# Row sums of a fused attention and SoLU kernel: 128x32 tiles of TensorE replaced by 64x64 tiles, and one PSUM copy per group of quads

## The chip, the cores and the metric

The kernel runs on one core of one Trainium2 chip. The metric is device time in microseconds (us) for one execution; the figure for a kernel is the median of several runs. The profile is one execution of its own, recorded by the hardware profiler, and its span is the time from the first to the last recorded event. Two of the chip's engines matter most below: TensorE (PE in the profile), which multiplies a stationary block of weights with a stream of moving columns and writes into the accumulator memory PSUM, and ScalarE (ACT), which takes exponentials and copies results out of PSUM. VectorE is DVE, GpSimd is POOL, SyncE is SP and issues most DMAs.

## The reference

Attention with normalised queries and keys, followed by a feed-forward block with a SoLU activation. For 8 batches of 12 heads, 448 tokens and 64 dimensions per head:

```
q_n, k_n = q / rms(q) * g_q, k / rms(k) * g_k
scores = q_n @ k_n.T / sqrt(64)
attn   = exp(scores - max) / (sum(exp(scores - max)) + 1e-9)     # sum over the keys
x      = attn @ v                                                # then (token, head*dim)
h      = x @ w_in                                                # 768 -> 1024
solu   = h * softmax(h);  ln = layernorm(solu) * g_ln
out    = ln @ w_out                                              # 1024 -> 768
```

Everything is float32. The change concerns only the sums over the keys, 8*12*448 numbers, by which the rows of the attention output are divided.

## The kernel before, in words

**Work and tiles.** The 96 heads are taken four at a time, a *quad*; there are 24 quads (`m` = 0 to 23), each with two pairs `i` of two heads `h`. For quads 1 to 23 the 448 keys are cut into seven blocks `kc` of 64. `both_scores` (line 870) makes the scores of one block for all four heads: four matmuls with 64 rows and 64 columns of weights and 448 moving columns (the queries), each in its own quarter of the 128x128 array, into one PSUM tile `s`. ScalarE turns the tile into exponentials `E` (the last block's are called `El`) in `exponentials` (line 833), with 128 partitions (64 keys of pair 0, then 64 keys of pair 1) times 2 heads times 448 queries. `both_values` (line 884) multiplies the same block by `v`, again four 64x64 matmuls, and accumulates over `kc` in the PSUM tile `o`. Quad 0 is built from other loads: its two pairs are taken one after the other in blocks of 128 keys (`scores`, `values`, lines 841 and 930), and only the last 64 keys of both share a tile (`scores_last`, `values_last`).

**Row sums.** The sums over keys are column sums of `E` over partitions. VectorE first adds some of the seven blocks elementwise into tiles `es` (`add_pair`, `add_to`), so that a quad has a short list of *terms*: five for quad 0, four for quads 1 and 2, three for each later quad (`El` and two `es`). Each term has a kind `w`: 2 means that its upper 64 partitions belong to pair 0 and its lower 64 to pair 1; 0 or 1 (quad 0 only) that all 128 belong to that pair. `sums` (line 941) lets TensorE do the rest with a stationary block of ones and zeros, `ones[:, w]`, of 128 rows and 32 columns: the first 16 columns give pair 0's sum and the last 16 pair 1's, each repeated 16 times. For each term there are four matmuls, one for each head `h` and each half `t` of the queries, with 224 moving columns, into four strips of 32 PSUM partitions.

`sums` runs once for a group of quads, nine times in all: after quad 0, after quads 1 and 2 together, and after each further three quads (`sums_at`, line 1458). I call each of the nine a *phase*. The quads of a phase land in different columns of the PSUM tile `sm`, so that `keep_sums` (line 957) needs one ScalarE copy for one or two quads and two copies for three, into `r`; one DMA then sends every sixteenth partition of `r` to DRAM (`sd`). Later the sums are loaded back, inverted and stored in `rd`, and `load_r` broadcasts them over the rows of x.

**What sets the order.** The whole order is written by hand in the body after line 1492. Each unit issues TensorE work, and the other engines' work stands between units. On TensorE a quad is four blocks of scores, then values and scores in turn, then four blocks of values. A phase of sums stands between the last values of a quad and the first scores of the next; in the phase after quads 1 and 2 a small transpose of the gains (`norm_gain`, line 477) follows the sums. `keep_sums` is called at the start of the next quad (line 1578), ahead of its exponentials on ScalarE; `send` comes after the DMAs that store the previous quad's output (line 1598). Three PSUM buffers of tag "t" are shared in turn by `s` and `sm` (and in the next stage by the products of `w_in`).

After the attention come the product with `w_in` (128x128 tiles, line 1103) with the activation behind it, and the product with `w_out` (line 1329), both by Strassen-like schemes on TensorE.

In the traces each matmul call of the code stands as two rows (float32 is streamed twice), so four calls are "x8".

Of the kernel before, what the change touches and what calls it, by code (L numbers as in the profile page):

```python
# [9 lines left out]
FP32 = mybir.dt.float32  # L10
# [356 lines left out]
def fast_path(  # L367
# [24 lines left out]
    nc = tc.nc  # L392
    B, H, S, D = q.shape
    DM, DFF = moe_w_in.shape
    P = 128
    NJ = S // P
# [24 lines left out]
    work = first.enter_context(tc.tile_pool(name="work", bufs=2))  # L421
# [1 line left out]
    w_out = conv = sums_in = None  # L423

    ident = consts.tile([P, P], FP32, name="ident")
    ones = work.tile([P, 3, 32], FP32, tag="ones", name="ones", bufs=1)

    w_in = {k: wi.tile([P, HD, DFF // 2], FP32, name=f"w_in{k}") for k in (0, 5, 1, 4, 3, 6, 2)}
    xd = [dram.tile([DM, S], FP32, name=f"xd{b}") for b in range(B)]
    sd = dram.tile([NQ, 8, S // 2], FP32, name="sd")  # L430
    rd = [dram.tile([NP // 2, 8, S // 2], FP32, name=f"rd{b}") for b in range(B)]
# [17 lines left out]
    def setup():  # L449
        nc.gpsimd.memset(mhalf, -0.5)  # L450
        nc.gpsimd.memset(seven, 7.0)
        nc.gpsimd.memset(eps, 1e-6)


        for i, x in enumerate((-1.9375, -1.00390625, -(0.1249 ** 2))):
            nc.gpsimd.memset(limits[:, i : i + 1], x)


        nc.gpsimd.memset(ones, 0.0)
        for i in range(2):  # L460
            c = slice(16 * i, 16 * i + 16)
            nc.gpsimd.memset(ones[:, i, c], 1.0)
            nc.gpsimd.memset(ones[i * D : (i + 1) * D, 2, c], 1.0)
        make_identity(nc, ident)

    def load_gains():
# [158 lines left out]
    st = {}  # L625
    quads = {}
# [303 lines left out]
    def values(n):  # L930


        d = st[n]
        for kc in range(NJ):
            for h in range(2):
                nc.tensor.matmul(
                    d["o"][h * D : (h + 1) * D, :], quads[n // 2]["v"][:, n % 2 + 2 * h, kc], d["E", kc][:, h],
                    start=False, stop=(kc == NJ - 1),
                )

    def sums(ms):


        sm = ps_t.tile([P, 2, 512], FP32, tag="t", name="sm")
        for j, m in enumerate(ms):
            terms = quads[m]["terms"]
            for x, (w, e) in enumerate(terms):
                for h in range(2):
                    for t in range(2):
                        g = 32 * (2 * h + t)  # L950
                        nc.tensor.matmul(  # L951
                            sm[g : g + 32, j % 2, j // 2 * S // 2 : (j // 2 + 1) * S // 2], ones[:, w], e[:, h, t * S // 2 : (t + 1) * S // 2],
                            start=(x == 0), stop=(x == len(terms) - 1),
                        )
        return sm

    def keep_sums(ms, sm):


        n = len(ms)  # L960
        r = work.tile([P, 3, S // 2], FP32, tag="r", name="r", bufs=1)
        w = min(n, 2)
        nc.scalar.copy(r[:, 0:w], sm[:, 0:w, 0 : S // 2])
        if n == 3:
            nc.scalar.copy(r[:, 2], sm[:, 0, S // 2 : S])

        def send():
            nc.sync.dma_start(sd[ms[0] : ms[0] + n].rearrange("j r c -> r j c"), r[0:P:16, 0:n])

        return send  # L970

# [46 lines left out]
    def load_r(g):  # L1018


        n = 2 if g == 0 else 1
        if g == 0:
            tiles = [work.tile([P, 2 * NB, 32], FP32, tag="qkn", name="r0", bufs=2).rearrange("p b d -> p (b d)") for _ in range(2)]
        else:
            tiles = [sums_in.tile([P, KD * 2 * P], FP32, tag="r", name="rg", bufs=1)]
        w = KD // n
        gs[g, "r"] = [x[:, 0 : w * 2 * P].rearrange("p (c t) -> p c t", c=w) for x in tiles]
        for i, x in enumerate(gs[g, "r"]):
            t = 2 * g * P
            while t < 2 * (g + 1) * P:  # L1030
                b, c = divmod(t, S)
                half, c = divmod(c, S // 2)
                k = min(S // 2 - c, 2 * (g + 1) * P - t)
                o = t - 2 * g * P
                for h in range(2):
                    r = rd[b].rearrange("j (h t i) c -> i t (j h) c", h=2, t=2, i=2)
                    r = r[h, half, i * w : (i + 1) * w, c : c + k]
                    nc.sync.dma_start(
                        x[h * D : (h + 1) * D, :, o : o + k], r.rearrange("c t -> () c t").to_broadcast([D, w, k])
                    )  # L1040
                t += k
# [181 lines left out]
    def in_parts():  # L1223
        def done(g, i):
            t = 2 * g + i
            ff_max(t)
            waits = {
                (NG - 2, 1): (1, 2, 3, 4, 5, 6), (NG - 2, 0): (2, 3, 4, 5, 6, 7.25),
                (NG - 1, 1): (1, 2, 4.5, 5, 7.25, 7.75), (NG - 1, 0): (2.25, 4.25, 5.25, 6, 7.5, 8.75),
            }.get((g, i), (1, 2, 3, 4, 5, 7) if i else (2, 3, 4, 6, 7, 9))  # L1230
            steps = (ff_exp, ff_mult, ff_deviations, ff_spread_of, ff_norm, ff_spread)
            for x, f in zip(waits, steps):
                later(x, lambda f=f: f(t))

        p = [products(g, lambda i, g=g: done(g, i)) for g in range(NG)]
        parts = [p[0][1], p[0][2]]
        for g in range(NG):
            turn = [p[g][6], p[g][5], p[g][7], p[g][4], p[g][3]]
            x = len(parts)
            if g + 1 < NG:  # L1240
                turn[4:] = [p[g + 1][1], p[g][3], p[g + 1][2]]
            parts += turn
            if g + 1 < NG:
                follow(parts, x + 1, lambda g=g: [scale(g + 1, i) for i in range(3)])
                if g + 2 < NG:
                    follow(parts, x + 2, lambda g=g: load_r(g + 2))
                    follow(parts, x + 3, lambda g=g: load_x(g + 2))
                follow(parts, x + 2, lambda g=g: sizes(g + 1))
                follow(parts, x + 2, lambda g=g: block_sums(g + 1, 0))
                follow(parts, x + (5 if g > 6 else 6), lambda g=g: block_sums(g + 1, 1))  # L1250
        return parts
# [189 lines left out]
    def unit(f, steps=4):  # L1441
        nonlocal now
        f()
        now += steps
        due = [x for x in todo if x[0] <= now]
        todo[:] = [x for x in todo if x[0] > now]
        for _, g in sorted(due, key=lambda x: x[0]):
            g()
# [23 lines left out]

    load_rows(0, (nc.sync, nc.sync, nc.scalar, nc.scalar))
    setup()
    load_gains()
    load_rows(1, (nc.sync, nc.sync, nc.scalar, nc.scalar))
# [15 lines left out]
    with tc.manual_schedule():  # L1492
# [53 lines left out]
        unit(lambda: values_last(0))  # L1546
        unit(lambda: values(0))
        unit(lambda: values(1))
        quads[0]["terms"] = [(2, quads[0]["E", NJ])]
        quads[0]["terms"] += [(0, st[0]["es"])] + [(1, st[1]["E", x]) for x in range(NJ)]  # L1550
        waiting = [0]

        def end_sums():
            sm = sums(waiting)
            return list(waiting), sm
# [5 lines left out]
        for m in range(1, NQ):  # L1561
            a, b = 2 * m, 2 * m + 1
# [14 lines left out]
            if kept:  # L1577
                sent = keep_sums(*kept)
                kept = None
# [132 lines left out]
            if m == NQ - 2:  # L1712
                load_x(0)
                load_r(0)
# [10 lines left out]
            if m in sums_at:  # L1725
                unit(lambda: None)
                kept = end_sums()
                waiting.clear()
        take(NQ - 1)
        sent = keep_sums(*kept)  # L1730
        store_x(NQ - 1)
        sent()
# [4 lines left out]
        parts_in = ExitStack()  # L1737
        sums_in = pool(parts_in, "sums_in")
        load_r(1)
        for _ in range(3):  # L1740
            load_next()
# [19 lines left out]
        for x in range(8, 44):  # L1761
            e = nc.vector if (44 + x) % 7 in (3, 5) else nc.gpsimd
# [28 lines left out]
        for n in range(NS):  # L1791
            base = period * n
            for i, name in enumerate(ORDER):
# [4 lines left out]
                x = HALVES[name][0]  # L1798
# [65 lines left out]
@with_exitstack  # L1864
def kernel(
    ctx: ExitStack,
    tc: tile.TileContext,
    q: bass.AP,
    k: bass.AP,
    v: bass.AP,  # L1870
    g_q: bass.AP,
    g_k: bass.AP,
    moe_w_in: bass.AP,
    moe_w_out: bass.AP,
    moe_g_ln: bass.AP,
    out: bass.AP,
):
    nc = tc.nc
    flags = ctx.enter_context(tc.tile_pool(name="flags", bufs=1))
    flag = flags.tile([1, 1], I32, name="flag")  # L1880
    large = flags.tile([1, 1], FP32, name="large")
    fast_path(tc, q, k, v, moe_w_in, moe_w_out, out, g_q, g_k, moe_g_ln, large)
    nc.vector.tensor_copy(flag, large)
    other = nc.values_load(flag[0:1, 0:1], min_val=0, max_val=1)
    with tc.If(other > 0):
        general_path(tc, q, k, v, g_q, g_k, moe_w_in, moe_w_out, moe_g_ln, out)
# [30 lines left out]
```

## Time and profile before

| | before |
|---|---|
| median of 3 runs | 782.74 us (782.05 to 783.13) |
| profiled execution, its own time | 781.84 us |
| its span | 780.0 us |
| PE busy | 771.0 us, 99% |
| DVE, ACT, POOL busy | 603.6, 508.9, 487.3 us |

A duration of one PE row is the time from its start to its modelled end; rows in different quarters of the array overlap, so what a group costs is read from the distance between the starts of groups. The chain of waits follows the work that ended last back to the start and so counts each moment once; its times stand some hundredths of a us off those of the timeline.

### The profile page before, as it was taken

The numbers are of one execution on the slowest core, as the hardware profiler recorded it, in microseconds if no ns is written. First come the engines' busy times: TensorE is split into PE (matmuls) and PEld (weight loads), VectorE is DVE, ScalarE is ACT, GpSimd is POOL, SyncE is SP. The second block draws the span as 40 slices with busy tenths as digits, with TensorE's granted clock in tenths as the row PEclk, the third lists the DMA queues.
The fourth block names the chain that finished last, engine by engine and source line by source line (L and its number), as shares of the span: only waits on it lengthen the run. The fifth ranks groups of instructions, "written<-read, shape, count | busy, mean of one in ns | idle before, by whom it ended". The sixth has DMA issues, their size and how long they took to land.

```text
span 780.0 us, 15087 instructions
## 1 busy us (share of the span) xinstructions
PE 771.0 (99%) x5262; PEld 478.3 (61%) x5262; DVE 603.6 (77%) x1064; ACT 508.9 (65%) x833; POOL 487.3 (62%) x635
## 2 busy tenths in 40 slices
PE   8999999999999999999999999999999999999997
PEld 4444445445454444444444444444899999999996
DVE  6878999999999983687777667685797695776844
ACT  6778898888989862787777656655626445464510
POOL 2565444455464552455687688888898787777862
PEclk9999999999999999999999999999999999999999
DMA  9999999999999367588887777773757647456312
GB/s 164 173 188 192 194 198 176 200 209 187 186 203 172 91 171 165 130 196 182 195 203 169 161 150 165 163 182 69 224 154 240 207 145 256 144 188 242 104 62 87
DMA packets 279818, 134.27 MB, mean 172 GB/s; under 512 B 190324, under 2 KB 264884, under 8 KB 279732
## 3 DMA queue, kind: packets, MB, share of 16 engines
q1 hardware_dynamic: 265892, 123.31, 70.4%
q10 hardware_dynamic: 13840, 9.90, 4.4%
q8 instruction: 44, 0.72, 0.4%
q14 instruction: 42, 0.34, 0.1%
HBM read 96.12 MB, written 37.04 MB: 171 GB/s over the span
## 4 chain that ended last, share of the span: by engine, by line
PE 94%; SPq 3%; DMA 1%; DVE 0%; POOL 0%; ACT 0%; issue 0%; POOLq 0%; ACTq 0%
PE A L1329 16%; PE o L891 15%; PE s L879 15%; PE A L1103 14%; PE B L1103 9%; PE B L1329 8%; PE D L1103 5%; PE C L1103 5%; PE C L1329 4%; PE sm L951 4%; SPq L647 2%; DMA qk<-in_k_dram 0%; DMA gg<-in_g_q_dram 0%; DVE part L696 0%; POOL ss L706 0%
## 5 line engine op out<-in xcount | busy, mean ns | idle before, releaser
L879 PE MATMUL s<-qkT 64*64 64x448 f32 x1288 | 139.3, 540 | 0.3 <-ACT qkT L745 0.2
L839 ACT ACTIVATE E<-s 128x896 f32<-128x896 f32 x144 | 124.5, 920 | 20.5 <-PE s L879 19.7
L729 POOL TENSOR_TENSOR qkn<-qk,ny 128x896 f32<-128x896 f32 x45 | 77.2, 1736 | 72.9 <-DVE ny L723 33.5
L891 PE MATMUL o<-E,v 64*64 64x448 f32 x1104 | 120.4, 536 | 0.0
L879 PEld LDWEIGHTS s<-qkT 64*64 64x64 f32 x1288 | 66.1, 191 | 60.0 <-issue 38.8
L1329 PE MATMUL A<-w_out,sums 128*128 128x192 f32 x392 | 79.8, 326 | 0.0
L1329 PE MATMUL B<-w_out,sums 128*128 128x192 f32 x392 | 79.8, 326 | 0.0
L891 PEld LDWEIGHTS o<-E,v 64*64 64x64 f32 x1104 | 42.4, 133 | 56.2 <-issue 49.0
L1103 PE MATMUL A<-w_in,xg 128*128 128x512 f32 x168 | 76.8, 593 | 0.0
L1103 PE MATMUL B<-w_in,xsum 128*128 128x512 f32 x168 | 76.7, 592 | 0.0
L1329 PEld LDWEIGHTS B<-w_out,sums 128*128 128x128 f32 x392 | 66.4, 190 | 0.0
L1329 PEld LDWEIGHTS A<-w_out,sums 128*128 128x128 f32 x392 | 66.4, 190 | 0.0
L750 DVE STREAM_TRANSPOSE qkT<-qkn 128x896 f32<-128x896 f32 x46 | 49.9, 1098 | 9.4 <-POOL qkn L729 9.4
L1103 PEld LDWEIGHTS B<-w_in,xsum 128*128 128x128 f32 x168 | 31.9, 190 | 40.2 <-issue 39.9
L1103 PEld LDWEIGHTS A<-w_in,xg 128*128 128x128 f32 x168 | 31.8, 190 | 40.1 <-issue 38.4
L905 DVE TENSOR_TENSOR es<-es,E 128x896 f32<-128x896 f32 x44 | 49.3, 1120 | 4.4
L1205 ACT ACTIVATE u<-u,shift,he 128x1024 f32<-128x1024 f32 x28 | 34.8, 1241 | 27.2 <-POOL shift L1201 27.1
L696 DVE TENSOR_REDUCE part<-sq 128x28 f32<-128x896 f32 x46 | 47.9, 1074 | 4.3 <-ACT sq L690 4.3
L1079 POOL TENSOR_TENSOR xsum<-xg 128x384 f32<-128x384 f32 x14 | 14.4, 1030 | 57.2 <-ACT xsum L1062 35.0
L899 DVE TENSOR_TENSOR es<-E 128x896 f32<-128x896 f32 x46 | 50.1, 1089 | 0.0
L1329 PE MATMUL A<-w_out,s 128*128 128x192 f32 x224 | 45.6, 326 | 0.0
L690 ACT ACTIVATE sq<-qk 128x896 f32<-128x896 f32 x45 | 41.0, 944 | 2.1 <-DMA qk<-in_k_dram 0.7
(173 smaller groups left out, 1655.4 us busy)
## 6 DMA issues: line engine op xcount, KB each, us to landing
ur<-ud SPq DMA_DIRECT2D x60, 256.0 KB, 4.7
ud<-ub SPq DMA_DIRECT2D x112, 128.0 KB, 2.8
xd<-xo SPq DMA_DIRECT2D x48, 224.0 KB, 4.2
qk<-in_q_dram SPq DMA_DIRECT2D x92, 112.0 KB, 4.2
qk<-in_k_dram SPq DMA_DIRECT2D x92, 112.0 KB, 4.0
v<-in_v_dram SPq DMA_DIRECT2D x23, 448.0 KB, 5.2
out_dram<-P SPq DMA_DIRECT2D x19, 384.0 KB, 4.0
raw<-in_moe_w_in_dram SPq DMA_DIRECT2D x12, 512.0 KB, 5.0
```

The lines of the kernel that those rows point to most:

```text
L690: nc.scalar.activation(d["sq"].rearrange("p (s b) d -> p s (b d)", s=2), d["qk"], AF.Square)
L696: nc.vector.tensor_reduce(norms[m]["part"][:, i], st[n]["sq"], AX, OP.add)
L729: e.tensor_tensor(d["qkn"].rearrange("p (s b) d -> p s b d", s=2), d["qk"].rearrange("p s (b d) -> p s b d", d=32), y.rearrange("p (s b) - ...
L750: nc.vector.transpose(d["qkT"].rearrange("p s t -> p (s t)"), d["qkn"].rearrange("p b d -> p (b d)"))
L839: nc.scalar.activation(e, s[:, :, 0:S], AF.Exp)
L879: nc.tensor.matmul(s[i * D : (i + 1) * D, h, 0:S], qkT[hh, i, 1, keys], qkT[hh, i, 0], start=True, stop=True)
L891: nc.tensor.matmul(d["o"][h * D : (h + 1) * D, i, 0:S], d["v"][pp, h, kc], d["E", kc][pp, h], start=kc == 0, stop=kc == NK - 1,)
L899: nc.vector.tensor_tensor(e, d["E", x], d["E", y], OP.add)
L905: engine.tensor_tensor(e, e, d["E", x], OP.add)
L1103: nc.tensor.matmul(k[bank], a[:, c], w_in[i][:, c], start=begin and c == 0, stop=c == HD - 1, skip_group_check=not begin,)
L1205: nc.scalar.activation(d["u"], d["u"], AF.Identity, scale=d["e"], bias=d["shift"])
L1329: nc.tensor.matmul(k[bank], a[:, c].rearrange("p a i -> p (a i)"), w_out[:, area, i, c], start=begin and c == 0, stop=c == KC - 1, skip_gr ...
```

## The change

The sums are made with the array tiling of scores and values. The stationary block is now 64 columns wide, and it is cut out of `ones` (112 columns, of which 48 to 63 are ones) at a place that depends on the quad's position `j` in its phase: its 16 columns of ones are columns 16j to 16j+15 of the block. So each quad of a phase writes its sums to PSUM rows of its own, and adds zeros to the others' rows; all quads of a phase accumulate in the same columns of `sm`. A term of kind 2 is four matmuls of 64 rows and 64 columns with 448 moving columns (head `h`, pair `i`), each pair in its own PSUM bank; a term of kind 0 or 1 (quad 0) is two matmuls of 128 rows and 64 columns. `keep_sums` makes one copy of 128 x 896 elements in every phase; `r` has no buffer of its own any more but takes its turn among the six `es` buffers. Two DMAs, one for each head, send the sums, and `load_r` reads the rows in the new order. GpSimd's setup has one memset of ones in place of four. For quad 0 the term `El` comes last instead of first.

```
-    ones = work.tile([P, 3, 32], FP32, tag="ones", name="ones", bufs=1)
+    ones = work.tile([P, 112], FP32, tag="ones", name="ones", bufs=1)
...
         nc.gpsimd.memset(ones, 0.0)
-        for i in range(2):
-            c = slice(16 * i, 16 * i + 16)
-            nc.gpsimd.memset(ones[:, i, c], 1.0)
-            nc.gpsimd.memset(ones[i * D : (i + 1) * D, 2, c], 1.0)
+        nc.gpsimd.memset(ones[:, 48:64], 1.0)
...
         sm = ps_t.tile([P, 2, 512], FP32, tag="t", name="sm")
+        runs = []
         for j, m in enumerate(ms):
-            terms = quads[m]["terms"]
-            for x, (w, e) in enumerate(terms):
+            w = ones[:, 48 - 16 * j : 112 - 16 * j]
+            for pair, e in quads[m]["terms"]:
                 for h in range(2):
-                    for t in range(2):
-                        g = 32 * (2 * h + t)
-                        nc.tensor.matmul(
-                            sm[g : g + 32, j % 2, j // 2 * S // 2 : (j // 2 + 1) * S // 2], ones[:, w], e[:, h, t * S // 2 : (t + 1) * S // 2],
-                            start=(x == 0), stop=(x == len(terms) - 1),
-                        )
+                    if pair < 2:
+                        runs.append((h, pair, w, e[:, h]))
+                        continue
+                    for i in range(2):
+                        pp = slice(i * D, (i + 1) * D)
+                        runs.append((h, i, w[pp], e[pp, h]))
+        for x, (h, i, w, e) in enumerate(runs):
+            same = [y for y, r in enumerate(runs) if r[:2] == (h, i)]
+            nc.tensor.matmul(sm[h * D : (h + 1) * D, i, 0:S], w, e, start=x == same[0], stop=x == same[-1])
         return sm
...
-        r = work.tile([P, 3, S // 2], FP32, tag="r", name="r", bufs=1)
-        w = min(n, 2)
-        nc.scalar.copy(r[:, 0:w], sm[:, 0:w, 0 : S // 2])
-        if n == 3:
-            nc.scalar.copy(r[:, 2], sm[:, 0, S // 2 : S])
+        r = work.tile([P, 2, S], FP32, tag="es", name="r", bufs=6)
+        nc.scalar.copy(r, sm[:, :, 0:S])
...
-            nc.sync.dma_start(sd[ms[0] : ms[0] + n].rearrange("j r c -> r j c"), r[0:P:16, 0:n])
+            rows = sd[ms[0] : ms[0] + n].rearrange("j (h r) c -> h j (r c)", h=2)
+            for h in range(2):
+                nc.sync.dma_start(rows[h], r[h * D : h * D + 16 * n : 16].rearrange("j i t -> j (i t)"))
...
-                    r = rd[b].rearrange("j (h t i) c -> i t (j h) c", h=2, t=2, i=2)
+                    r = rd[b].rearrange("j (h i t) c -> i t (j h) c", h=2, t=2, i=2)
...
-        quads[0]["terms"] = [(2, quads[0]["E", NJ])]
-        quads[0]["terms"] += [(0, st[0]["es"])] + [(1, st[1]["E", x]) for x in range(NJ)]
+        quads[0]["terms"] = [(0, st[0]["es"])] + [(1, st[1]["E", x]) for x in range(NJ)]
+        quads[0]["terms"] += [(2, quads[0]["E", NJ])]
```

The order of the instructions on TensorE, ScalarE and SyncE can be read from the two built kernels (lines between 459 and 955 stand up to three lines higher or some lines lower in the changed file; x4 is four calls).

TensorE around quad 0's phase, before; `vl` and `v` are values, `sm` the sums:

```order
L849 MATMUL s<-qkT 64x448 x12
L925 MATMUL o<-El,vl 64x448 x4
L936 MATMUL o<-E,v 64x448 x12
L951 MATMUL sm<-El,ones 32x224 x4
L951 MATMUL sm<-es,ones 32x224 x4
L951 MATMUL sm<-E,ones 32x224 x12
L879 MATMUL s<-qkT 64x448 x16
```

The same place in the changed kernel:

```order
L846 MATMUL s<-qkT 64x448 x12
L922 MATMUL o<-El,vl 64x448 x4
L933 MATMUL o<-E,v 64x448 x12
L955 MATMUL sm<-es,ones 64x448 x2
L955 MATMUL sm<-E,ones 64x448 x6
L955 MATMUL sm<-El,ones 64x448 x4
L876 MATMUL s<-qkT 64x448 x16
```

`El` has gone from the head of the sums to their end, and the 20 calls of 32 x 224 have become 12 of 64 x 448. In the later phases nothing changes its place: each term keeps its four calls, with 64 x 448 in place of 32 x 224.

ScalarE around the first phase of three quads, before; `sq` are squares for a later quad, `r` the copied sums:

```order
L714 ACTIVATE ny<-ny 128x56
L690 ACTIVATE sq<-qk 128x896 x2
L963 COPY r<-sm 128x448
L965 COPY r<-sm 128x224
L839 ACTIVATE E<-s 128x896 x5
L538 ACTIVATE tmp<-raw,seven 128x512
```

The same place in the changed kernel:

```order
L711 ACTIVATE ny<-ny 128x56
L687 ACTIVATE sq<-qk 128x896 x2
L963 COPY r<-sm 128x896
L836 ACTIVATE E<-s 128x896 x5
L535 ACTIVATE tmp<-raw,seven 128x512
```

Two copies of 672 elements per partition together have become one of 896, at the same place ahead of the exponentials.

## Prediction

> **What bounds the kernel now.** I read the page's busy times and its chain by engine first, then a table of windows, then the groups of the sums' line, then the chain and the timeline around the phases.
>
> ```profile
> span 780.0 us, 15087 instructions
> PE 771.0 (99%) x5262; PEld 478.3 (61%) x5262; DVE 603.6 (77%) x1064; ACT 508.9 (65%) x833; POOL 487.3 (62%) x635
> PE 94%; SPq 3%; DMA 1%; DVE 0%; POOL 0%; ACT 0%; issue 0%; POOLq 0%; ACTq 0%
> ```
>
> TensorE is busy for 771.0 of 780.0 us and makes 94% of the chain that ended last. A busy TensorE could still be one that idles inside a stage, so here is the bulk of the attention stage, in the table of windows (window, its length, then the busy time of PE, PEld, DVE, ACT and POOL, the granted clock, the DMA share and GB/s):
>
> ```profile
> 121.60:295.00 173.40, 173.39 (x1973) 84.46 (x1969) 160.26 (x206) 146.37 (x201) 89.63 (x118) 1.00 0.90 178
> ```
>
> TensorE idles 0.01 us in 173.40, at clock 1.00. The other engines have slack. Whatever TensorE is given more to do in this stage, it does on the critical path.
>
> The sums' line in the groups by form (tiles, shape, count, then busy time and mean ns of one):
>
> ```profile
> L951 PE MATMUL sm<-es,ones 128*32 128x224 f32 x376 | 22.2, 352 | 0.0
> L951 PE MATMUL sm<-El,ones 128*32 128x224 f32 x192 | 13.7, 357 | 0.0
> L951 PE MATMUL sm<-E,ones 128*32 128x224 f32 x40 | 2.4, 352 | 0.0
> ```
>
> That is 608 rows, 8 for each term: 76 terms (5 for quad 0, 2 x 4, 21 x 3). How fast a term goes shows in the timeline of TensorE at the first phase of three quads, and in the chain (start, length, what; the first and the last of the six such phases inside the stage, and two stretches of scores with no sums ahead of them):
>
> ```profile
> 81.83 0.93 PE L891 MATMUL o<-El,v 64*64 64x448 f32 x8
> 82.69 0.59 PE L951 MATMUL sm<-El,ones 128*32 128x224 f32 x8
> 83.10 0.94 PE L951 MATMUL sm<-es,ones 128*32 128x224 f32 x16
> 83.85 0.56 PE L951 MATMUL sm<-El,ones 128*32 128x224 f32 x8
> ```
>
> ```profile
> 82.76 3.54 PE sm L951 x72
> 86.31 3.23 PE s L879 x32
> ...
> 97.05 3.01 PE s L879 x32
> ...
> 107.58 3.01 PE s L879 x32
> ...
> 259.43 3.54 PE sm L951 x72
> 262.97 3.23 PE s L879 x32
> ```
>
> Two terms of the old sums take 83.85 - 83.10 = 0.75 us, so one takes 0.375. A group of four 64x64 matmuls with 448 columns, which is what scores and values are, takes 3.01 / 4 = 0.7525 us. Both run four tiles side by side at the same rate for each column; the old tiles simply have half the columns.
>
> **The main term: the stream.** In the new form a term of kind 2 is four 64x64 matmuls with 448 columns: the tiling, the shape and the mapping (64 rows of one pair, 64 columns of one head, one PSUM bank for each pair) of `both_values`. I therefore charge 0.7525 us in place of 0.375. The 64 columns of weights hold 16 of use and the array is held twice as long.
>
> **What goes with the old tiling.** At both ends of a phase there is a gap where the tiling changes. The last values of the quad start at 81.83 and need 0.7525, so the sums could start at 82.58 and start at 82.69: 0.11 us. The first term takes 0.41 instead of 0.375. The scores behind the phase take 3.23 in the chain, and 3.01 where no sums are ahead of them: 0.22. The whole phase costs 3.54 + 3.23 - 3.01 = 3.76 us, of which 9 x 0.375 = 3.38 are stream and 0.38 the two changes.
>
> For these gaps the Trainium skill has a rule that speaks for the change: TensorEngine Tiling (Array Packing), Key Properties, says that a change of tiling mode, not merely of tile, drains TensorE. The trace agrees, with the 0.11 and 0.22 us above, and the page gives no price. With these gaps as a drain's price the sum comes to the 25.7 us below; by the rule taken without them, with a drain of unknown size, to anything under the 28.7 us of bare stream.
>
> After the change there is no gap and nothing but stream: 9 x 0.7525 = 6.77 us. So each of the six phases of three quads inside the stage costs 6.77 - 3.76 = 3.01 us more: 18.06 us for six.
>
> The other three phases have other neighbours:
>
> ```profile
> 47.32 3.16 PE sm L951 x64
> ...
> 295.07 3.54 PE sm L951 x72
> 298.61 2.77 PE A L1103 x6
> 301.38 2.58 PE C L1103 x6
> ```
>
> ```profile
> 18.38 4.73 PE L936 MATMUL o<-E,v 128*64 128x448 f32 x24
> 23.04 0.59 PE L951 MATMUL sm<-El,ones 128*32 128x224 f32 x8
> ...
> 25.07 3.30 PE L879 MATMUL s<-qkT 64*64 64x448 f32 x32
> 28.19 0.93 PE L891 MATMUL o<-E,v 64*64 64x448 f32 x8
> ```
>
> The last phase is followed by the 128x128 tiles of `w_in`, whose first group pays for the change of tiling (2.77 against 2.58) with either form, so I leave that: 6.77 - 3.54 = 3.23 us. The phase after quads 1 and 2 has eight terms and is followed by the transposes of the gains, so the change behind it stays too: 8 x 0.7525 - 3.16 = 2.86 us. Quad 0's phase follows values in 128x64 tiles: 24 rows, six terms' worth, 4.52 us, so they end at 22.90 and the sums start 0.14 late. They last to 25.07, 2.03 us, and the scores behind take 3.12 instead of 3.01. In the new form four of the five terms are pairs of 128x64 matmuls with 448 columns, at the rate of L936, which is again 0.75 us each, and there is no change ahead of them; but with `El` moved to the end the change to 64x64 comes before `El` and keeps its 0.11. So 5 x 0.7525 - 2.03 - 0.14 = 1.59 us.
>
> Sum on TensorE: 18.06 + 3.23 + 2.86 + 1.59 = 25.74 us.
>
> **What hides some of it.** Only the first quads are not bound by TensorE alone; the chain reaches TensorE there at 38.76, out of a load:
>
> ```profile
> 25.92 3.65 DMA qk<-in_k_dram
> ...
> 38.76 1.04 PE s L879 x8
> ```
>
> ```profile
> 36.12 3.69 PE L879 MATMUL s<-qkT 64*64 64x448 f32 x32 [0.24 <-ACT qkT L745]
> ```
>
> From 25.07 to 36.12 to 47.32 quads 1 and 2 take 11.05 and 11.20 us, against 10.53 for a later quad (107.58 - 97.05). Less the 0.11 of the tiling, 1.08 us are waits. A later TensorE can hide between nothing of it and all of it: nothing, since ScalarE, which feeds those scores, works in order behind exponentials that move with TensorE; all of it, if only the loads set the pace. I take the one wait that stands in a row, 0.24 us.
>
> **ScalarE's copy.** In place of 448 and 224 columns it copies 896, ahead of the next quad's exponentials:
>
> ```profile
> 86.37 0.53 ACT L963 COPY r<-sm 128x448 f32<-128x448 f32 x1 [0.63 <-PE sm L951]
> 86.80 0.35 ACT L965 COPY r<-sm 128x224 f32<-128x224 f32 x1
> 87.34 3.35 ACT L839 ACTIVATE E<-s 128x896 f32<-128x896 f32 x4 [0.19 <-PE s L879]
> 88.32 0.50 PEld L879 LDWEIGHTS s<-qkT 64*64 64x64 f32 x8 [0.25 <-ACT E L839]
> ```
>
> 448 columns take 0.18 us more than 224, so 896 take about 0.53 + 0.36 = 0.89 (an estimate), and the copies, from 86.37 to 87.15 before, become 0.11 longer. Ahead of the first exponential ScalarE still waits 0.19 for scores, and this covers it. If the cover is gone, the fourth block of scores (last row) waits for the first exponential to free its PSUM tile, and TensorE pays up to 0.11 us nine times, 1.0 us; nothing below zero, since no copy becomes shorter. I take 0.
>
> **DMA, GpSimd, buffers.** SyncE issues nine more DMAs:
>
> ```profile
> 90.37 0.61 SPq L968 DMA_DIRECT2D sd<-r  x1
> ```
>
> ```profile
> 305.68 2.01 DVE L1051 TENSOR_TENSOR xg<-xg,rg 128x384 f32<-128x384 f32 x3 [0.87 <-issue]
> ```
>
> ```profile
> 314.25 2.58 PE A L1103 x6
> ```
>
> Queued behind the second one are the loads of later quads, and in the last phase the loads of `rg`; they start 0.61 us later. The scaling of x by `rg` ends at 307.69 and TensorE needs it at 314.25: 6.6 us of cover, so 0 (at worst 0.61 where no cover is left). The `es` buffer that `r` used is written again in the third quad after, at 107 us or later, some 17 us after the DMA's issue, against 3.65 for the landing above: 0. GpSimd's setup loses three memsets:
>
> ```profile
> 4.75 0.31 POOL L486 TENSOR_TENSOR gg<-gg 1x64 f32<-1x64 f32 x1 [2.84 <-DMA gg<-in_g_k_dram]
> ```
>
> Behind it GpSimd waits 2.84 us for a load anyway: 0.
>
> **The number.** 25.74 - 0.24 = 25.5 us. The profiled execution took 781.84 us and would take 807.3. The median of the runs before, 782.74, is 0.9 above it; on that footing the forecast is **808.2 us**, 3.3% slower.
>
> **The rivals.**
>
> *The start swallows the early phase.* Up to 38.76 us the chain runs through loads; if these alone set the pace, quad 0's 1.59 us are hidden, and with them 0.1 us here and there in the next quads. For it speaks that chain, against it ScalarE's order. It gives 25.74 - 1.59 - 0.3 = 23.8, so 806.6 us.
>
> *The new tiles do not run four wide.* If the two pairs' tiles came one after the other, a term would take 1.505 us, another 76 x 0.7525 = 57.2 us: 865.4 us. It would decide if the pairs' row tiles got into each other's way at PSUM. Against it: `both_values` writes the same partitions and banks from the same tiles at 0.7525.
> The Trainium skill has a rule for this case: by TensorEngine Tiling (Array Packing), Gotcha 1: PSUM Pressure, different row tiles cannot access one PSUM bank at the same time. Here the pair selects the bank, so by that rule, too, nothing is held up.
>
> *Not slower: the changes of tiling are dearer than the gaps show.* The change takes away two in each of six phases and one in each of the other three, 15 in all. To pay for 76 x 0.3775 = 28.7 us of stream each would have to cost 1.9 us; the time would then be 782.7. The rows price one at 0.11 to 0.22, and the six phases' whole excess over their stream is 0.38 each. What could still make it so is time that the modelled ends put down to the neighbours.
>
> **How the numbers follow.** Forecast 0.80, early phase swallowed 0.13, not four wide 0.03, not slower 0.03, and 0.01 for something slower that I do not see. The range holds the first two: from 806.0 (806.6 less the 0.6 by which runs before scatter) to 810.0 (808.2 with the copy's 1.0, a late DMA's 0.6 and 0.2 of rounding). Faster or slower by over 0.2% (1.6 us, about what a measurement can tell here): slower 0.97, the sum of all but the third rival; that one is split into 0.01 within 0.2% and 0.02 faster.
>
> **What would show it.** Each row of the sums at 64*64 and 64x448; three terms' starts 2.26 us apart; the chain with 6.8 us of sums at each phase of three quads, scores behind it back at 3.01, and the sums' share at about 7% of the span. The first product of `w_in` starts 25 us later, at about 324, and what follows keeps its length. It would be wrong if sums took 1.1 us or more for a term, if scores behind a phase stayed at 3.23 or grew (ScalarE's copy), or if the stages after the attention changed their length.

## The result, and the profile after

The changed kernel takes 808.73 us (median; 808.51 to 809.07), the kernel before beside it 782.39 (781.76 to 783.21). The ratio is 1.0336, with a 95% interval from 1.0322 to 1.0349: 26.3 us slower, and 0.5 us from the forecast of 808.2.

The profiled execution took 808.51 us. The head of its page, the largest row of the sums' line in the groups by form, and TensorE's timeline in the first phase of three quads:

```profile
span 806.7 us, 15054 instructions
PE 796.2 (99%) x5246; PEld 482.3 (60%) x5246; DVE 605.4 (75%) x1064; ACT 510.1 (63%) x826; POOL 483.1 (60%) x632
PE 95%; DVE 2%; POOL 1%; DMA 1%; ACT 1%; issue 0%; SPq 0%; POOLq 0%; DVEq 0%; ACTq 0%
```

```profile
L955 PE MATMUL sm<-es,ones 64*64 64x448 f32 x368 | 38.7, 536 | 0.0
```

```profile
86.31 0.93 PE L888 MATMUL o<-El,v 64*64 64x448 f32 x8
87.06 0.93 PE L955 MATMUL sm<-El,ones 64*64 64x448 f32 x8
87.82 1.68 PE L955 MATMUL sm<-es,ones 64*64 64x448 f32 x16
89.32 0.93 PE L955 MATMUL sm<-El,ones 64*64 64x448 f32 x8
```

Three terms start 2.26 us apart (89.32 - 87.06), 0.753 each. And the values that start at 86.31 give way to sums after 0.75 us, with no gap for a change of tiling. In the chain, the phases (that of quads 1 and 2, the first and the last of the six of three quads inside the stage, then the last one) and the first product of `w_in`:

```profile
48.96 6.01 PE sm L955 x64
...
87.24 6.76 PE sm L955 x72
94.01 3.01 PE s L876 x32
...
278.92 6.76 PE sm L955 x72
...
317.25 6.76 PE sm L955 x72
324.02 2.77 PE A L1103 x6
```

Each phase of three quads now takes 6.76 us, and the scores behind it are back at 3.01. The same points in both chains tell where the time came from. A phase that began at 47.32 begins 1.64 us later (48.96), the one at 82.76 is 4.48 late (87.24), the one at 259.43 is 19.49 late (278.92): 3.00 for each of the five phases between. The last phase is 22.18 late (295.07, now 317.25), and the first product of `w_in` 25.41 (298.61, now 324.02). The 476 us behind that keep their length: the last add on VectorE, in its timeline in the kernel before and after, is late by the same 25.41.

```profile
774.48 0.36 DVE L1391 TENSOR_TENSOR P<-B,u 128x192 f32<-128x192 f32 x1 [0.29 <-PE B L1329]
```

```profile
799.89 0.36 DVE L1391 TENSOR_TENSOR P<-B,u 128x192 f32<-128x192 f32 x1 [0.29 <-PE B L1329]
```

One difference is left, and it lies behind all the work. From the end of that add to the end of the span it is 780.0 - 774.84 = 5.16 us before, and 806.7 - 800.25 = 6.45 after. Of the span's 26.7 us, then, 25.4 come from TensorE and 1.3 from this last stretch, which I had not priced.

### The profile page after: what moved, and what is told of

It is laid out like the page before. It is cut to its first block, busy times and chain, and to the rows that moved or that the text cites. A ratio compares the mean times of both kernels' runs of the same rounds, so it can differ in the third digit from the quotient of the medians.

```text
span 806.7 us, 15054 instructions
## 1 busy us (share of the span) xinstructions
PE 796.2 (99%) x5246; PEld 482.3 (60%) x5246; DVE 605.4 (75%) x1064; ACT 510.1 (63%) x826; POOL 483.1 (60%) x632
## 4 chain that ended last, share of the span: by engine, by line
PE 95%; DVE 2%; POOL 1%; DMA 1%; ACT 1%; issue 0%; SPq 0%; POOLq 0%; DVEq 0%; ACTq 0%
PE A L1329 16%; PE o L888 14%; PE s L876 14%; PE A L1103 13%; PE B L1103 9%; PE B L1329 8%; PE sm L955 7%; PE C L1103 4%; PE D L1103 4%; PE C L1329 4%; DMA xd<-xo 0%; DVE part L693 0%; DMA x<-in_q_dram 0%; POOL ss L703 0%; POOL qkn L726 0%; PE s L846 0%
## 5 line engine op out<-in xcount | busy, mean ns | idle before, releaser
L1079 POOL TENSOR_TENSOR xsum<-xg 128x384 f32<-128x384 f32 x14 | 14.7, 1050 | 61.2 <-ACT xsum L1062 47.5
```

## The experiments

My theory: the sums cost what TensorE streams, twice the columns for each term, less the old changes of tiling. The rivals: the new tiles are slow for another reason (not four wide, or ScalarE's longer copy holds the scores), or the changes of tiling are worth much more than their gaps. And for the 1.3 us at the end: SyncE's nine further DMAs, or something else that the change moved. Each kernel is compared with the kernel before on the same chip; its interval is that of the ratio.

**Half the columns in the new tiles** (of the kernel after; a term streams 224 of its 448 columns, so half of the sums' work is left out).

```
+            part = same.index(x) % 2
+            t = slice(part * S // 2, (part + 1) * S // 2)
-            nc.tensor.matmul(sm[h * D : (h + 1) * D, i, 0:S], w, e, ...
+            nc.tensor.matmul(sm[h * D : (h + 1) * D, i, t], w, e[:, t], ...
```

> The changed kernel, with each matmul of the sums streaming 224 columns in place of 448: of each region's terms every second one covers the first half of the queries and the others the second half, so half of the row sums' work is left out. Tiles, calls and weights stay as they are. If the cost is the stream of columns, a term takes 0.376 us in place of 0.7525, the 76 terms give back 28.6 us, and the time is 808.7 - 28.6 = 780.1 us, some 2.3 below the kernel before, which has the same stream and the changes of tiling besides. If the 64x64 form is dear in itself (its calls, its weights, its row tiles), the time stays near 808.7. If changes of tiling are dear (1.9 us each, 15 of them), the time falls to about 754, since this kernel has the old stream without them.

Measured: 782.93 us, ratio 1.001 [1.0, 1.0019]. Its chain, at some phases and between two of them, and the bulk of its attention stage in the table of windows:

```profile
83.02 3.40 PE sm L957 x72
86.43 3.01 PE s L876 x32
...
118.07 3.40 PE sm L957 x72
...
153.04 3.40 PE sm L957 x72
...
223.28 3.40 PE sm L957 x72
...
239.42 1.09 DVE xo L991
...
240.56 0.98 PE o L888 x8
...
258.83 3.40 PE sm L957 x72
```

```profile
126.00:300.00 174.00, 173.15 (x1997) 87.42 (x1990) 159.11 (x202) 143.22 (x192) 88.75 (x112) 1.00 0.88 173
```

A phase is at 3.40 us, nine times 0.375 and 0.02 more, so inside a phase the tiles, weights and banks of the new form cost nothing by themselves; the stream does. The total is 2.8 us above what I had expected, though. 1.3 us of it is the last stretch again (6.42 us). The rest lies between phases. From 118.07 to 153.04 it is 34.97 us; from 223.28 to 258.83 it is 35.55, and the chain leaves TensorE there and comes back to it out of VectorE at 240.56; to the next phase, at 294.55, it is 35.72. That is 1.3 us in two places. The window (columns as in the prediction's) has VectorE busy for 159.11 of 174.00 us and TensorE idle for 0.85: with shorter phases the other engines come into reach. Some 0.2 us of the 2.8 stay unexplained.

**The old tiles, streamed twice** (of the kernel before; each matmul twice, the block of ones at 0.5; the listing leaves out the memsets and the `start` and `stop` of the pair).

```
...
             for x, (w, e) in enumerate(terms):
-                for h in range(2):
+                for twice in range(2):
+                  for h in range(2):
...
```

> The kernel before, with every matmul of the sums made twice and halves for ones, so that the sums stay the same. The tiling and its changes stay as they are and the stream doubles. If the stream is the cost: 782.4 + 76 x 0.376 = 811.0 us, a little above the changed kernel. If the changed kernel's loss came from its 64x64 tiles and not from the columns, this one stays much nearer to 782.4 than to 808.7.

Measured: 810.11 us, ratio 1.0353 [1.0336, 1.0371]. Its chain:

```profile
87.68 6.95 PE sm L952 x144
94.63 3.23 PE s L879 x32
```

The old tiling with as many columns costs as much as the new one, and a little more, which fits the gaps that it keeps: 6.95 + 3.23 - 3.01 = 7.17 us for a phase against 6.76. The last stretch is 5.02 us here, with no more DMAs than before.

**The price of a change of tiling.** Both kernels add to the kernel before, ahead of the second and third quad of each phase (15 places), four small matmuls of 64 columns into unused PSUM: in the first in 64x64 tiles, so that the tiling changes twice more at each place, and in the second in 128x32, the tiles that are there anyway.

```
+            if j:
+                for h in range(2):
+                    for i in range(2):
+                        pp = slice(i * D, (i + 1) * D)
+                        nc.tensor.matmul(sm[h * D : (h + 1) * D, i, S : S + D], ident[pp, 0:D], ident[pp, D:P], ...
...
```

> The kernel before, with one group of four 64x64 matmuls of 64 columns (on constants, into unused columns of the PSUM tile, read by nobody) between the quads of a phase: 15 groups in all, each of which changes the tiling there and back. By the gaps of the trace a pair of changes costs 0.38 us, and the group's stream 0.11: 782.4 + 15 x 0.49 = 789.8 us. If a change of tiling costs 1.9 us, as it would have to for the changed kernel to break even: 782.4 + 15 x 3.9 = 841.

```
+            if j:
+                for g in range(0, P, 32):
+                    nc.tensor.matmul(sm[g : g + 32, 0, S : S + D], ident[:, 0:32], ident[:, D:P], ...
...
```

> The control of the run with switches: the same 15 groups, of four matmuls of 64 columns, but in the 128x32 tiles of the sums, so that the tiling never changes. Stream alone, 0.11 us each: 782.4 + 1.6 = 784.0 us. The difference to the run with switches is the price of 15 pairs of changes: 5.7 us by the gaps, 57 if they are dear.

Measured: 787.88 us (1.0072 [1.0055, 1.0089]) and 783.46 us (1.0014 [1.0004, 1.0024]). The same phase in the two chains, first with the changes, then without:

```profile
83.30 1.27 PE sm L959 x24
84.57 0.28 PE sm L950 x8
...
87.66 3.23 PE s L879 x32
```

```profile
82.97 1.27 PE sm L957 x24
84.25 0.11 PE sm L948 x8
...
86.74 3.23 PE s L879 x32
```

Four changes more lengthen the phase from 3.77 to 4.36 us, 0.29 for a pair, and the totals say the same: 4.42 / 15 = 0.29. That is a bit below the 0.38 of the two gaps in the prediction. A pair would have to cost 3.8 us for the rival in which the change is not slower.

**ScalarE's copy twice** (of the kernel after).

```
         nc.scalar.copy(r, sm[:, :, 0:S])
+        nc.scalar.copy(r, sm[:, :, 0:S])
```

> The changed kernel with ScalarE's copy of the sums made twice, which shows how thick the cover of the copy is. The first exponential behind a phase starts 0.9 us later; the fourth block of scores waits for the PSUM tile that it frees and has about 0.2 us of room, so TensorE loses about 0.6 us in each of the eight phases that scores follow: 808.7 + 5 = 814 us. If the copy has ample cover: 808.7.

Measured: 815.32 us, ratio 1.0424 [1.0409, 1.0438], 6.6 us above the kernel after, or 0.82 for each of eight phases. TensorE's timeline behind a phase in this kernel, and ScalarE's in the same place:

```profile
95.75 1.68 PE L876 MATMUL s<-qkT 64*64 64x448 f32 x16
97.90 1.87 PE L876 MATMUL s<-qkT 64*64 64x448 f32 x16 [0.46 <-ACT r L964]
```

```profile
96.00 0.91 ACT L963 COPY r<-sm 128x896 f32<-128x896 f32 x1 [4.13 <-PE sm L955]
96.94 0.91 ACT L964 COPY r<-sm 128x896 f32<-128x896 f32 x1
```

One copy is hidden, a second one isn't. The wait is not the one that I had named. It is the third block of scores, which waits for the copy itself because it takes over the PSUM tile of `sm`, not the fourth block for the first exponential. Two blocks give it 1.5 us, until 97.25; one copy ends at 96.91. The third block starts at 97.90, 0.65 us late, and the two blocks behind the wait need 1.68 us (to 99.58) in place of 1.5; together these are the 0.82. So the cover of the copy is only about 0.3 us.

**Where the last stretch comes from.** First the sums in the old tiles but with the new form's layout by shifted ones: all three quads in one bank, one copy of 224 columns, one DMA for each quad (24 in place of 9, of the kernel before).

```
...
+            nc.gpsimd.memset(ones[:, i, 16 * i : 16 * i + 4], 1.0)
+            for j in range(3):
+                c = slice(16 * i + 4 * j, 16 * i + 4 * j + 4)
+                nc.gpsimd.memset(ones[i * D : (i + 1) * D, 2 + j, c], 1.0)
...
-                            sm[g : g + 32, j % 2, j // 2 * S // 2 : (j // 2 + 1) * S // 2], ones[:, w], ...
+                            sm[g : g + 32, 0, 0 : S // 2], ones[:, w + j], ...
...
+        nc.scalar.copy(r, sm[:, 0, 0 : S // 2])
...
+            for j in range(n):
+                nc.sync.dma_start(sd[ms[0] + j], r[4 * j : P : 16])
```

> The other parts of the change without its tiles: the kernel before with its 128x32 tiles, but a block of ones shifted for each quad, so that all quads of a phase have rows of their own and keep_sums makes one copy, here of 224 columns; one DMA for each quad sends the sums, 24 in all in place of 9. If tiles are all that counts and the rest is covered: 782.4 us within 0.5. If the number of copies or DMAs mattered: off by 1 us or more.

Measured: 784.05 us, ratio 1.0024 [1.0015, 1.0034]. The last add begins at 774.26, 0.2 us earlier than before, and the last stretch is 6.68 us. So the layout costs TensorE nothing, and the loss lies at the program's end alone. Next, the kernel after with one DMA for each phase in place of two (`sd` is made three quads longer, since the DMA always sends four):

```
...
-            rows = sd[ms[0] : ms[0] + n].rearrange("j (h r) c -> h j (r c)", h=2)
-            for h in range(2):
-                nc.sync.dma_start(rows[h], r[h * D : h * D + 16 * n : 16].rearrange("j i t -> j (i t)"))
+            rows = sd[ms[0] : ms[0] + 4].rearrange("j (h r) c -> h j (r c)", h=2)
+            nc.sync.dma_start(rows, r[0:P:16].rearrange("p i t -> p (i t)"))
```

> The changed kernel with one DMA for each phase in place of two: it sends four rows for each head, the last ones of no use, which later phases write over. SyncE's program is then as long as before. If that sets the end of the span: the last addition stays at 800.3 within 0.3 and the time falls by 1.3 us, to 807.4. If not: 808.7.

Measured: 807.37 us, ratio 1.0321 [1.0307, 1.0335]. VectorE's last add, from the timeline:

```profile
799.94 0.36 DVE L1390 TENSOR_TENSOR P<-B,u 128x192 f32<-128x192 f32 x1 [0.29 <-PE B L1328]
```

TensorE ends where it did in the kernel after (0.05 us later), the span is 805.5 us, and the last stretch is back at 5.20 us. Then the other way round: the kernel before, with its one send made twice.

```
-            nc.sync.dma_start(sd[ms[0] : ms[0] + n].rearrange("j r c -> r j c"), r[0:P:16, 0:n])
+            for _ in range(2):
+                nc.sync.dma_start(sd[ms[0] : ms[0] + n].rearrange("j r c -> r j c"), r[0:P:16, 0:n])
```

> The kernel before, with the DMA that sends the sums issued twice, so that SyncE has nine more DMAs in its program, as in the changed kernel. TensorE's work is the same. In the runs so far the stretch from the last addition on VectorE to the end of the span is 5.0 to 5.3 us in the kernels with SyncE's program as before, and 6.4 to 6.7 us in all that have more DMAs on SyncE (the changed kernel among them). If the longer program on SyncE is what makes it, the last addition stays at 774.8 within 0.3, and the time rises by 1.3 us, to 783.6. If the end is longer for another reason that the changed kernels share, the time stays at 782.3.

Measured: 793.66 us, ratio 1.0155 [1.0132, 1.0178], much too slow, and useless for the question. The waits of SyncE's queue (in total, times, longest) show why:

```profile
SPq L969 <- DMA sd<-r: 22.5, 9, 3.9
```

The second write goes to the same place, and the built program lets it wait on SyncE for the first one to land (18 semaphore waits on this line, nine more than there are phases), with the loads of later quads behind it. So I sent the second copy to a DRAM tile of its own:

```
...
+    spare = dram.tile([NQ, 8, S // 2], FP32, name="spare")
...
+            for x in (sd, spare):
+                nc.sync.dma_start(x[ms[0] : ms[0] + n].rearrange("j r c -> r j c"), r[0:P:16, 0:n])
```

> The kernel before, with a second DMA in each phase that sends the sums to a spare place in DRAM that nobody reads, so that it has no earlier DMA to wait for (in the run with the sends doubled SyncE waited 22.5 us in all for the first of each two to land). SyncE's program is nine DMAs longer. If its length sets the end of the span: the last addition within 0.3 us of 774.8 and 6.4 to 6.7 us behind it, so 783.6 us. If the end depends on something else in the changed kernels: 5.2 us behind it, 782.3. If even an extra DMA on SyncE with nothing to wait for pushes loads back: more than 784.

Measured: 783.12 us, ratio 1.0016 [1.0007, 1.0025]. The last add:

```profile
774.53 0.36 DVE L1393 TENSOR_TENSOR P<-B,u 128x192 f32<-128x192 f32 x1 [0.29 <-PE B L1331]
```

TensorE's work ends where it does in the kernel before (774.48 there), and the span, 781.0 us, is 1.0 longer: the last stretch is 6.11 us. Nine DMAs more on SyncE add 1.0 to 1.3 us behind the end of the work; that is shown, by adding them and by taking them away.

Where the time goes shows in the semaphore instructions with which SyncE closes the program. Here are eight of them, of the kernel after in the windows 804 to 805 and 805 to 806 us, and of the kernel before in the window 778.5 to 779.2 (count, shortest, median and longest in ns, first and last start):

```profile
L1912 SPq EVENT_SEMAPHORE  x5: 28/28/28, 804.2 to 804.5; - x5
L1912 SPq EVENT_SEMAPHORE  x3: 28/28/28, 805.7 to 805.8; - x3
```

```profile
L1912 SPq EVENT_SEMAPHORE  x8: 28/28/28, 778.7 to 779.2; - x8
```

Before, the eight start within 0.5 us. After, SyncE pauses for 1.15 us behind the fifth. Counting SyncE's instruction records in the traces of all fourteen kernels of this study tells when that happens. Ahead of the closing instructions every kernel waits 2.6 to 2.9 us. Behind that wait, the seven kernels that have 902 records show no gap over 0.43 us on SyncE, and they end 5.0 to 5.3 us behind their last add. The other seven have 910, 911, 917 or 918 records; all of them pause, for 1.13 to 2.03 us, and always behind the 903rd record, which is not the same instruction in these four programs. They need 6.1 us or more. So the place in SyncE's stream decides, and not what the next instruction waits for: the nine DMAs cost time because they push the end of SyncE's program past that place.

What makes SyncE pause there stays open. A block of instructions that is fetched too late would fit a pause at a fixed place, but this is only argued. The packets of the queue that carries instructions, q14, do not show it. Up to the end of the span the pages count 42 of them in the seven kernels without the pause and 43 in the seven with it, but that is because the shorter spans end before the last packet. In windows of 17 us around the end (766.0 to 783.0 of the kernel before, 792.7 to 809.7 of the kernel after) both have eight (packets, MB, share):

```profile
q14 instruction: 8, 0.07, 1.3%
```

```profile
q14 instruction: 8, 0.07, 1.2%
```

From the start of the span to the end of the record all fourteen have 43. A rule of the Trainium skill speaks against a late fetch: Runtime: NRT & Kernel Launch, Instruction fetch mechanics, says that instructions are refilled in blocks and that the cost of a further block is mostly hidden. If the pause is such a refill, it was not hidden here; whether it is one, no run here shows.

**Fewer terms.** If columns are what sums cost, a term less saves TensorE 0.375 us in the old tiles and 0.75 in the new ones. In 14 quads that don't end a phase, GpSimd adds one term into another ahead of the sums, so that these stream two in place of three; first at once, in both kernels:

```
...
+                    if m not in sums_at:
+                        _, e = quads[m]["terms"].pop()
+                        s = quads[m]["terms"][0][1]
+                        nc.gpsimd.tensor_tensor(s, s, e, OP.add)
```

> The kernel before, with GpSimd adding the second es tile of a quad to its first, for the 14 quads from 3 on that are not the last of their phase: these have two terms in place of three. If a term costs 0.376 us of TensorE's time: 782.4 - 5.3 = 777.1 us. If GpSimd's 2 us of adding come in the way of the next quad's normalisation, or slow VectorE, the gain goes: 782 or more.

> The changed kernel with the same 14 additions on GpSimd. If a term costs 0.7525 us here: 808.7 - 10.5 = 798.2 us, twice the gain of the same edit in the old tiles. If terms are not what costs, less than that, down to none.

Measured: 805.28 us in the old tiles (1.03 [1.0286, 1.0314]) and 811.92 in the new (1.0379 [1.0365, 1.0393]). The term is saved, as a phase of seven terms in the chain of the second kernel shows (5.26 against 6.76 us), but the sum of the whole isn't:

```profile
128.01 5.26 PE sm L955 x56
```

In the first kernel TensorE is busy for only 166.12 of 179.00 us in the stage, at a granted clock of 0.97 on average, as the table of windows has it (what the clock alone costs I did not separate), and the row of GpSimd's add in the groups tells what it stands behind:

```profile
121.00:300.00 179.00, 166.12 (x1816) 76.83 (x1812) 165.25 (x202) 139.24 (x193) 100.39 (x119) 0.97 0.86 158
```

```profile
L1699 POOL TENSOR_TENSOR es<-es 128x896 f32<-128x896 f32 x14 | 31.7, 2265 | 54.3 <-DVE es L899 47.5 <-DVE nx L720 4.6 <-DMA qk<-in_q_dram 2.2
```

GpSimd's fourteen adds wait 47.5 us in all for VectorE's add of the same quad, and the next quad's normalisation waits behind it in order. Placed one quad later, where its operands are long done:

```
+                if m > 3 and m - 1 not in sums_at:
+                    _, e = quads[m - 1]["terms"].pop()
+                    s = quads[m - 1]["terms"][1][1]
+                    nc.gpsimd.tensor_tensor(s, s, e, OP.add)
```

> The kernel before with the 14 additions on GpSimd made one quad later, behind the next quad's normalisation and sums of squares, so that nothing that the next scores need stands behind a wait for VectorE. If only the place was wrong in the run that had them earlier, the terms saved show: 782.4 - 14 x 0.376 = 777.1 us. If GpSimd's 2 us beside VectorE slow the latter, or push the next normalisation back, the gain is eaten: 780 to 800.

Measured: 806.62 us, ratio 1.0311 [1.0297, 1.0325]. No better, and the traces point to another reason. The timeline of GpSimd and VectorE, at two quads, and the stage in the table of windows:

```profile
85.86 3.00 POOL L1683 TENSOR_TENSOR es<-es 128x896 f32<-128x896 f32 x1
86.84 2.97 DVE L899 TENSOR_TENSOR es<-E 128x896 f32<-128x896 f32 x1
...
108.56 2.10 POOL L1683 TENSOR_TENSOR es<-es 128x896 f32<-128x896 f32 x1
108.63 2.98 DVE L899 TENSOR_TENSOR es<-E 128x896 f32<-128x896 f32 x1
111.72 1.09 DVE L905 TENSOR_TENSOR es<-es,E 128x896 f32<-128x896 f32 x1
```

```profile
121.00:300.00 179.00, 164.91 (x1828) 75.68 (x1826) 169.10 (x203) 140.42 (x195) 100.84 (x119) 1.00 0.85 158
```

An add on VectorE that takes 1.09 us alone takes 2.97 and 2.98 beside GpSimd's. With it VectorE comes to 169.10 busy us of 179.00, and TensorE's waits for VectorE's copies of values and for the two engines' sums grow to some 22 us (13.3, 5.6 and 2.8). The Trainium skill has the rule: SBUF — State Buffer, SBUF: two separate sides, says that VectorE and GpSimd share a pair of ports by an exclusive lock, which holds for a VectorE operation with two inputs in SBUF beside GpSimd. The rows agree: GpSimd's adds end at 88.86 and 110.66, VectorE's, 0.95 us behind each of them. So no version beats the kernel that it was made from. That the slowed adds cost all of the time in this last one is argued from these rows; no run separates them from the other waits.

## Why the prediction held, step by step

- *The main term, the stream.* Right: 0.753 us for a term, and its two controls (half the columns, the old tiles twice) take the cost away and bring it back.
- *What goes with the old tiling.* Right in place and about in size: behind a phase the scores fell from 3.23 to 3.01 us, a middle phase costs 3.00 us more (forecast 3.01), the phase of quads 1 and 2 2.85 (2.86), and the last 3.23 (3.23). Behind quad 0's phase TensorE is 1.58 us late (1.59): the values that started at 28.19 start at 29.77, in TensorE's timeline of the kernel after:

```profile
25.96 0.98 PE L955 MATMUL sm<-El,ones 64*64 64x448 f32 x8
26.76 3.19 PE L876 MATMUL s<-qkT 64*64 64x448 f32 x32
29.77 0.93 PE L888 MATMUL o<-E,v 64*64 64x448 f32 x8
```

  A pair of changes measured by itself is 0.29 us.
- *What hides some of it.* Wrong place, and the right size by luck. I had put 0.24 us in the first quads. There nothing was hidden: the 1.58 us behind quad 0's phase are 1.64 at the next one. But in the last quads 0.31 us went: the six phases would make the last one 22.49 late (19.49 + 3.00), and it is 22.18 late. The chain of the kernel before has what went: two blocks of values take 0.98 us (at 283.50, behind ScalarE's last exponentials) and 0.82 (at 287.49), the others 0.75; in the kernel after all blocks of the last quad take 0.75. TensorE's sum is so 25.41 us, against 25.5.
- *ScalarE's copy.* 0, as said. The wait behind it is another one, and its cover, 0.3 us, is thinner than I had thought.
- *DMA, GpSimd, buffers.* This is the term that was mis-sized. On the way the nine DMAs cost nothing, as argued, and I had bounded them by 0.61 us for a late load. They cost 1.0 to 1.3 us at the end of the program, where I had looked at nothing, because they push SyncE's instructions past the place at which it pauses. With that term the sum would have been 25.4 + 1.3 = 26.7 us.
- *The number.* On the footing of the profiled executions the forecast was 807.3, and 808.51 came: 0.1 too much on TensorE and 1.3 too little at the end. Against the medians it is only 0.5 low, and that is luck, because the 0.9 that I had added for the runs before is more than the 0.2 by which the median after (808.73) stands above its profiled execution.
- *The rivals.* The start swallowed nothing. The tiles run four wide (a term at 0.753, not 1.505). A change of tiling costs some 0.15 us (half a pair), not 1.9.

## What to carry to other kernels

On a saturated TensorE, price a matmul by the columns that it streams for one pass of the array, whatever share of rows and weights is of use: two tilings that fill the array alike differ by the columns for each term (here 0.375 us for 224 and 0.753 for 448), and a change of tiling cost tenths of a microsecond here. Before moving work from such an engine to another, look at the busy share of that one in the same stage, and at which engine it shares a path with; the folds failed there. And compare the time behind the last useful instruction as well: it belongs to the span, and a few more instructions on an engine far from the critical path can lengthen it.

## What the runs showed of the hardware that I had not expected

- SyncE paused for 1.13 to 2.03 us behind the 903rd record of its instructions in all seven kernels whose SyncE program went on that far into its closing part, and in none of the seven that have 902 records. With it the stretch behind the last work is 6.1 to 7.4 us, without it 5.0 to 5.3; more DMAs issued hundreds of microseconds before are enough for the change. What makes SyncE pause stays open.
- A VectorE add of 128x896 took 1.09 us alone and up to 2.98 us beside an add on GpSimd.
- A second write to the same place in DRAM was built with a wait for the first to land, which took up to 3.9 us (2.5 us on average over nine) and held SyncE's queue.
